# A pre-norm attention and gated MLP block on one core: the exponentials of the last keys on VectorE as three shifted terms

## The chip, the core and the metric

The kernel runs on one core of a Trainium2 chip. TensorE multiplies matrices into PSUM, ScalarE takes exponentials, VectorE and GpSimd work element by element, and SyncE issues nearly all DMAs. The metric is the device time of one launch in microseconds (us), the median of the runs.

## The reference

One transformer block over 2048 rows of width 640, in bfloat16, with 32 heads of 20 columns:

```python
def _A_ref(x, wqkv, wo):
    qkv = (x @ wqkv).reshape(B, S, 3, H, Dh) ...
    scores = jnp.einsum("bhqd,bhkd->bhqk", q, k) * (Dh ** -0.5)
    p = _softmax(scores, axis=-1)
    o = jnp.einsum("bhqk,bhkd->bhqd", p, v)
    return o ... .reshape(B, S, D) @ wo
def _B_ref(x, w_gate, w_up, w_down):
    return ((x @ w_gate) * (x @ w_up)) @ w_down
h = x + _A_ref(_layernorm(x), wqkv, wo)
out = h + _B_ref(_layernorm(h), w_gate, w_up, w_down)
```

The hidden width of the second part is 1728.

## The kernel before

The 2048 queries are four blocks of 512 (block 0 to block 3), the heads eight groups of four. One **segment** is a block or half a block of queries with one group of heads; it runs over all 16 key tiles of 128 keys. Blocks 1, 2 and 3 take their first 4, 2 and 2 groups whole and the others in halves of 256 queries (passes C and D, E and F, A and B), so that the rows of a first half can go on early. A **unit** is one key tile (two in a half) by one head, 128 x 512 scores, one bank of PSUM.

Most units go to ScalarE: three and two banks in turn make a score tile `sc`, one activation turns it into `E`. The rest go to VectorE, 12 of the 64 units of a whole segment (`D_WHOLE`) and 6 of the 32 of a half (`D_HALF`), the last ones in key order. There the exponential is built from integer bits: a `TENSOR_SCALAR` from PSUM into `di` (L744), and for each pair of units three operations more (`dm` L627, `dt` L629, their product L632). `dt` and `di` are two terms whose sum is the exponential, so TensorE multiplies both with V into `acc` (L871). The sums of each row come from a column of ones in V; `norm` sends them through DRAM, takes their inverse on GpSimd (`rr`, L769), spreads it (`bc`) and scales there (L784).

When a block's or a half's groups are normed, its **tail** follows as jobs in one queue: `load`, `out` (output product, residual, layer norm, transposes), `glu` (up and gate products with weights `wu`, `wg`, or `wres` that stay in SBUF) and `y` (down product, store). Block 0 has one tail of 512 rows, the others have tails of 256 rows, and the last 256 rows have `last_tail` after everything.

All instructions are written out once by a planner that keeps clocks for the engines (`clk`). Per score tile `emit_S` issues scores and activation, then `fill_step` issues products with V and pieces of jobs on TensorE until shortly before ScalarE will want the next scores; where there is nothing to do, `idle_products` issues products that are thrown away. So each engine's order is fixed before the run. What is still in the queue after the last score tile comes out behind it, ahead of `last_tail`. `by_cols` splits TensorE work into strips of 32 columns.

Of the kernel before, what the change touches and what calls it, by code (L numbers as in the profile page):

```python
# [18 lines left out]
P = 128  # L19
# [25 lines left out]
D_WHOLE = (12, 12, 12, 12)  # L45
# [19 lines left out]
EXP_BIAS = KAPPA - 127.0 * math.log(2.0)  # L65
DB = 2
# [21 lines left out]
def kernel(  # L88
# [178 lines left out]
    clk = {"pe": 0.0, "dve": 0.0, "acc": 0.0, "kind": None, "piece": ROUND}  # L267
# [155 lines left out]
    TAILS = [(0, list(range(TPB)), [("0", range(NG))])]  # L423
# [21 lines left out]

    a_units, d_units, due, left = [], [], [], {}
    for s, (p, g, lo, hi, _) in enumerate(segs):
# [10 lines left out]
        left[s] = [n * (sum(u[2] == j for u in units) + sum(u[2] == j for u in own)) for j in range(HPG)]  # L458

    LAST_B, LAST_T = NB - 1, [2, 3]  # L460
    first_b = [next(k for k, u in enumerate(us) if all(PASS[segs[v[0]][0]][0] == LAST_B for v in us[k:])) for us in (a_units, d_units)]
    pos = {"a": 0, "d": 0}
# [15 lines left out]
    dve_now = {"tile": None, "n": 0, "us": [], "key": 0}  # L478
# [163 lines left out]

    def step_dq():
# [31 lines left out]
    def take(i):  # L675
# [4 lines left out]
        if late_d and (not wide or due[di] + 4 <= ia):  # L680
            when = max(clk["pe"], act_end.get(i - 2, 0))
            ok = next_free() < when + 200 or due[di] + LEAD < ia
            for k in range(di, di + 4):
                if ok and k < len(d_units) and d_units[k][0] == d_units[di][0] and all(d_units[k][2] != u[2] for u in us):
                    d_units[di], d_units[k] = d_units[k], d_units[di]
                    d = d_units[di]
                    pos["d"] += 1
                    break
# [3 lines left out]
    def emit_S(i):  # L692
# [9 lines left out]
        if d and dve_now["tile"] is None:  # L702
# [39 lines left out]
        if d:  # L742
# [87 lines left out]
    def when(u):  # L830
        return u[0] if u[4][0] == "d" else act_end[u[0]] + WAKE

    def pick(s, i, flush, need):
        units = list(av_d[s]) + list(av_a[s])
        fit = lambda u: u[0] <= (clk["pe"] if u[4][0] == "d" else i - 2)
# [5 lines left out]
        for u in first + rest:  # L841
            if u[2] not in seen and len(got) < HPG:
                seen.add(u[2])
                got.append((av_d[s] if u[4][0] == "d" else av_a[s], u))
        return got

    def emit_AV(i, rounds, flush=False, need=None):
        while rounds > 0 and acc["next"] < len(segs):
# [15 lines left out]
            for q, u in got:  # L864
                q.remove(u)
                _, kt, j, e, owner = u
# [231 lines left out]

# [3 lines left out]
    def open_late():  # L1102
# [6 lines left out]
        late["s"] = pool("ls", 2, side="right")  # L1109
        late["if"] = late["s"].tile([P, P], F32, name="identf", bufs=1)  # L1110
# [9 lines left out]
    def new_st(rows_of):  # L1120
        hp = late["h"]
        st = {"rows": rows_of, "xr": {}}
        st["ln2T"] = hp.tile([P, KT, QB], BF16, name="ln2T")
        st["hh"] = [hp.tile([P, 2, QB], BF16, name=f"hh{f}") for f in range(FP)]
# [436 lines left out]
```

## Time and profile before

| what | value |
|---|---|
| runs | 876.83, 881.02, 881.36 us; median 881.02 |
| profiled execution, span from first to last instruction | 875.8 us, mean granted clock 0.991 |
| its own time beside the span | not among the times shown; the runs lie 1.0 to 5.6 us above the span |
| busy: TensorE, ScalarE, VectorE, GpSimd | 827.1, 799.6, 701.5, 191.0 us |
| exponentials on ScalarE | 679 activations, the first at 29.14 us, the last ending at 820.8 us |
| units on VectorE | 350 in 175 pairs |

Line numbers (L744) are those of the kernel before. In rows of groups the columns are: line, engine, operation, output and inputs, shapes, count, then busy time in us and mean ns of one, then the idle time before them and what ended it. In rows of the timeline: start and length in us, engine, line, operation, count; an entry in brackets is idle time before. In rows of windows: the stretch, its length, busy time and count of each engine, the granted clock, the share of the DMA engines and GB/s. A busy TensorE row is not TensorE at its peak, since its matmuls overlap; times per matmul are therefore read from rows of weight loads (PEld) in an unbroken run.

### The profile page before, as it was taken

The numbers are of one execution on the slowest core, as the hardware profiler recorded it, in microseconds if no ns is written. First come the engines' busy times: TensorE is split into PE (matmuls) and PEld (weight loads), VectorE is DVE, ScalarE is ACT, GpSimd is POOL, SyncE is SP. The second block draws the span as 40 slices with busy tenths as digits, with TensorE's granted clock in tenths as the row PEclk, the third lists the DMA queues.
The fourth block names the chain that finished last, engine by engine and source line by source line (L and its number), as shares of the span: only waits on it lengthen the run. The fifth ranks groups of instructions, "written<-read, shape, count | busy, mean of one in ns | idle before, by whom it ended". The sixth has DMA issues, their size and how long they took to land.

```text
span 875.8 us, 34459 instructions
## 1 busy us (share of the span) xinstructions
PE 827.1 (94%) x15313; PEld 406.3 (46%) x15313; DVE 701.5 (80%) x1384; ACT 799.6 (91%) x711; POOL 191.0 (22%) x259
## 2 busy tenths in 40 slices
PE   8899999998999999999999999999999999999995
PEld 5334334332334334445444555655454556555774
DVE  6675778899778989888888888989988898788632
ACT  5899999999999999999999999999999999899530
POOL 2220001344413322212230223122310232014000
PEclk9999999999999999999999999999999999899998
DMA  6111230144222322101314031413510310031310
GB/s 183 35 59 52 68 98 3 44 120 114 53 67 53 115 74 76 39 9 39 98 40 128 24 98 45 117 31 97 127 34 23 99 48 15 17 93 48 82 46 18
DMA packets 93959, 57.62 MB, mean 66 GB/s; under 512 B 24236, under 2 KB 91692, under 8 KB 93804
## 3 DMA queue, kind: packets, MB, share of 16 engines
q1 hardware_dynamic: 93804, 55.36, 23.7%
q8 instruction: 121, 1.98, 0.9%
q14 instruction: 34, 0.28, 0.1%
HBM read 46.94 MB, written 8.16 MB: 63 GB/s over the span
## 4 chain that ended last, share of the span: by engine, by line
PE 46%; ACT 25%; DVE 19%; issue 5%; DMA 2%; SPq 1%; POOL 1%; ACTq 0%; DVEq 0%; POOLq 0%
ACT E L732 25%; PE sc L724 11%; PE acc L871 9%; PE mi L286 9%; PE mi L1214 8%; DVE di L744 5%; PE mi L360 3%; DVE di L632 2%; DVE dm L627 2%; DVE st L219 2%; PE f L286 2%; PE f L1214 2%; DVE dt L629 2%; PE mi L724 1%; PE acc L1421 1%
## 5 line engine op out<-in xcount | busy, mean ns | idle before, releaser
L732 ACT ACTIVATE E<-sc 128x1536 bf16<-128x1536 f32 (+1 forms) x679 | 782.5, 1271 | 23.6 <-PE sc L724 10.6
L744 DVE TENSOR_SCALAR di<-mi 128x512 int16<-128x512 f32 x350 | 238.1, 685 | 65.9 <-PE mi L724 61.8
L871 PE MATMUL acc<-E,vx 128*32 128x256 bf16 (+1 forms) x2532 | 221.4, 315 | 2.6 <-DVE vx L257 2.0
L724 PE MATMUL sc<-qa,kT 21*128 21x256 bf16 (+1 forms) x1800 | 205.2, 320 | 15.0 <-ACT E L732 10.1
L724 PEld LDWEIGHTS <-kT 21*128 21x128 bf16 x3072 | 85.6, 92 | 218.9 <-issue 208.7
L769 POOL TENSOR_TENSOR rr<-rr,powers 128x8 f32<-128x8 f32 (+1 forms) x44 | 95.9, 2180 | 407.0 <-DMA rr<-sums 406.9
L871 PEld LDWEIGHTS <-vx 128*32 128x32 bf16 x3612 | 81.5, 95 | 105.7 <-issue 95.0
L632 DVE TENSOR_TENSOR di<-di,dm 128x1024 bf16<-128x1024 bf16 x175 | 122.2, 698 | 4.6
L724 PE MATMUL mi<-qa,kT 21*128 21x256 bf16 (+1 forms) x376 | 98.0, 311 | 2.4 <-DVE di L744 1.3
L627 DVE TENSOR_SCALAR dm<-di 128x1024 int16<-128x1024 int16 x175 | 77.7, 444 | 3.7
L871 PE MATMUL acc<-dt,vx 128*32 128x256 bf16 (+1 forms) x540 | 78.1, 311 | 0.5 <-DVE dt L629 0.4
L871 PE MATMUL acc<-di,vx 128*32 128x256 bf16 (+1 forms) x540 | 77.8, 308 | 0.8 <-DVE di L632 0.6
L629 DVE TENSOR_SCALAR dt<-di 128x1024 int16<-128x1024 int16 x175 | 76.2, 436 | 0.0
L724 PE MATMUL sc<-qb,kT 21*128 21x256 bf16 (+1 forms) x732 | 67.1, 291 | 2.8 <-ACT E L732 2.4
L286 PE MATMUL mi<-wd,hh 128*32 128x320 bf16 x1344 | 63.5, 305 | 0.4 <-DVE hh L1239 0.2
L1214 PE MATMUL mi<-ln2T,wg 128*32 128x256 bf16 (+1 forms) x1170 | 55.6, 298 | 1.9 <-DVE di L744 1.0
L1214 PE MATMUL mi<-ln2T,wu 128*32 128x256 bf16 (+1 forms) x1170 | 54.6, 298 | 0.9 <-DVE di L744 0.5
L286 PEld LDWEIGHTS <-hh 128*32 128x32 bf16 (+1 forms) x1456 | 46.1, 98 | 18.0 <-issue 7.5
L1214 PEld LDWEIGHTS <-wg 128*32 128x32 bf16 (+1 forms) x1190 | 32.6, 96 | 13.7 <-issue 10.0
L286 PE MATMUL mi<-kT,ident 128*32 128x512 bf16 x528 | 37.0, 382 | 1.7 <-DVE di L744 1.6
L1214 PEld LDWEIGHTS <-wu 128*32 128x32 bf16 (+1 forms) x1190 | 32.4, 96 | 13.3 <-issue 9.3
L257 DVE CAST u<-mi 128x512 bf16<-128x512 f32 x49 | 33.5, 683 | 4.9 <-PE mi L1214 4.8
(134 smaller groups left out, 794.1 us busy)
## 6 DMA issues: line engine op xcount, KB each, us to landing
wu<-in_B_w_up_dram SPq DMA_DIRECT2D x29, 320.0 KB
wg<-in_B_w_gate_dram SPq DMA_DIRECT2D x29, 320.0 KB
dense<-dn SPq DMA_DIRECT2D x36, 128.0 KB
bc<-scr SPq DMA_DIRECT2D x64, 64.0 KB
bc<-scr SPq DMA_DIRECT2D x112, 32.0 KB
xr<-in_A_x_dram SPq DMA_DIRECT2D x16, 160.0 KB
out_dram<-xr SPq DMA_DIRECT2D x14, 160.0 KB
wd<-in_B_w_down_dram SPq DMA_DIRECT2D x13, 160.0 KB
```

The costliest lines, as they stand in the source:

```text
L257: nc.vector.tensor_copy(dst, src)
L286: nc.tensor.matmul(out[k:k + w, :], lhsT=lhsT[:, k:k + w], rhs=rhs, **flags)
L360: nc.tensor.matmul(ps[k:k + SLOT, :], lhsT=wqk_half(c, col // HALF)[:, m, col % HALF:col % HALF + SLOT], rhs=lnT[:, c, ch * QB:(ch + 1) * ...
L627: nc.vector.tensor_scalar(m16[:, 0:n], s16, M_MASK, M_BITS, ALU.bitwise_and, ALU.bitwise_or)
L629: nc.vector.tensor_scalar(t16[:, 0:n], s16, E_MASK, E_BITS, ALU.bitwise_and, ALU.bitwise_or)
L632: nc.vector.tensor_tensor(sb[:, 0:n], sb[:, 0:n], mb[:, 0:n], ALU.mult)
L724: nc.tensor.matmul(dst[:, h * w:(h + 1) * w], lhsT=kT[g][SLOT * j:SLOT * j + VS, (kt + h) * P:(kt + h + 1) * P], rhs=q_of(g, b, c0, w)[SLO ...
L732: nc.scalar.activation(e[:, 0:n], sc[:, 0:n], ACT.Exp, bias=EXP_BIAS, scale=SM_SCALE)
L744: nc.vector.tensor_scalar(t[:, k * BANK:(k + 1) * BANK], sd[:], EXP_A, 0.0, ALU.mult, ALU.max)
L769: nc.gpsimd.tensor_tensor(ri, r16, powers[:, 1:2].to_broadcast([P, n]), ALU.pow)
L871: nc.tensor.matmul(acc["t"][SLOT * j:SLOT * (j + 1), 0:w], lhsT=vx[kt][:, VS * h:VS * h + SLOT], rhs=e, start=(j not in acc["new"]), stop= ...
L1214: nc.tensor.matmul(ps[r0 + x:r0 + x + d, col:col + n], lhsT=wt[:, c, f0 + x:f0 + x + d], rhs=st["ln2T"][:, c, c0:c0 + n], start=(c == 0), ...
```

## The change

In blocks 1 and 2 the exponentials of key tiles 14 and 15 that go to VectorE are made in another way: VectorE makes one integer tile `pt`, GpSimd adds 42 and 85 to it for two more terms, and all three, read as bfloat16, are multiplied with copies of V that carry a weight each. GpSimd writes these weighted copies once, after block 0's scores, into the space of block 0's queries. That is 48 of the units of whole segments and 80 of the halves, 128 in all; 246 stay with the old way. Whole segments of blocks 1 and 2 give VectorE 16 units in place of 12, 24 more in all. The rule by which a tile picks its VectorE unit looks further ahead. Block 0's tail becomes two of 256 rows, buffers of the tails shrink to that, their opening moves ahead of block 1, and the resident weights wait until block 2's products with V are done.

```diff
-D_WHOLE = (12, 12, 12, 12)
+D_WHOLE = (12, 16, 16, 12)
+STEPS = (0, 42, 85)
+WEIGHTS = (0.478515625, 0.3828125, 0.30859375)
+SUM_T = (14, 15)
+SUM_B = (1, 2)
+SUM_BUFS = 3
+POOL_ADD = 650
...
-    TAILS = [(0, list(range(TPB)), [("0", range(NG))])]
+    TAILS = [(0, [2 * k, 2 * k + 1], [("0", range(NG))]) for k in range(2)]
...
+    def summed(u):
+        s, kt, j = u
+        return PASS[segs[s][0]][0] in SUM_B and kt in SUM_T
...
+    def scale_values():
+        for kt in SUM_T:
+            for k, w in enumerate(WEIGHTS):
...
+                    nc.gpsimd.tensor_scalar(qa_all[:, g, x:x + n * VS], vx[kt][:, h * VS:(h + n) * VS], w, None, ALU.mult)
...
+    def three_terms(t, u, key):
...
+        clk["pool"] = max(clk["pool"], clk["dve"] + 150)
+        for k in range(3):
+            if k:
+                nc.gpsimd.tensor_scalar(t[:, k, :], t[:, 0, :], STEPS[k], None, ALU.add)
+                clk["pool"] += POOL_ADD
+            at = clk["pool"] if k else clk["dve"]
+            for h in range(BANK // w):
+                av_d[s].append((at + 250, kt + h, j, t[:, k, h * w:(h + 1) * w].bitcast(BF16), ("p", key), k))
...
+        three = d and summed(d)
+        if three:
+            ensure(("open",))
+            p_key = dve_now["p"] = dve_now["p"] + 1
+            free_of(("p", p_key - SUM_BUFS))
+            t3 = late["p"].tile([P, 3, BANK], I16, name="pt", bufs=SUM_BUFS)
...
+        if three:
+            nc.vector.tensor_scalar(t3[:, 0, :], sd[:], EXP_A, 0.0, ALU.mult, ALU.max)
+            ev(BANK)
+            three_terms(t3, d, p_key)
...
+                v = scaled(u[5], kt, h) if len(u) > 5 else vx[kt][:, VS * h:VS * h + SLOT]
                 nc.tensor.matmul(
-                    acc["t"][SLOT * j:SLOT * (j + 1), 0:w],
-                    lhsT=vx[kt][:, VS * h:VS * h + SLOT], rhs=e,
+                    acc["t"][SLOT * j:SLOT * j + v.shape[1], 0:w], lhsT=v, rhs=e,
...
-        if not seen["last"] and pos["a"] >= first_b[0] and pos["d"] >= first_b[1]:
+        if not seen["last"] and pos["a"] >= first_b[0] and pos["d"] >= first_b[1] and acc["next"] >= last_seg:
```

How instructions move, at three places (line numbers after the change are higher; buffer numbers stand behind the names). First GpSimd, from the norm of block 0's last group into block 1. Before, with the inverse (`rr`), the scaling into `on` or `part` and the note of the sums:

```order
L769 TENSOR_TENSOR rr_4742<-rr_4742,powers_186 128x16
L784 TENSOR_TENSOR on7_145<-asb1_4740,bc0_4989 128x512
L753 TENSOR_TENSOR seen_sums_109<-seen_sums_109,rr_4742 128x32
L1113 MEMSET wd13_5233 64x640
L1125 MEMSET hh6_5242 64x512
L769 TENSOR_TENSOR rr_5166<-rr_5166,powers_186 128x16
```

The same place on GpSimd after the change, where `pt` are the tiles of three terms:

```order
L830 TENSOR_TENSOR rr_4796<-rr_4796,powers_186 128x16
L679 TENSOR_SCALAR pt_4927<-pt_4927 128x512 x2
L679 TENSOR_SCALAR pt_4953<-pt_4953 128x512 x2
L679 TENSOR_SCALAR pt_4970<-pt_4970 128x512 x2
L679 TENSOR_SCALAR pt_5009<-pt_5009 128x512 x2
L679 TENSOR_SCALAR pt_5029<-pt_5029 128x512 x2
L679 TENSOR_SCALAR pt_5051<-pt_5051 128x512 x2
L679 TENSOR_SCALAR pt_5073<-pt_5073 128x512 x2
L679 TENSOR_SCALAR pt_5090<-pt_5090 128x512 x2
L845 TENSOR_TENSOR on7_145<-asb1_4794,bc0_5063 128x512
L814 TENSOR_TENSOR seen_sums_109<-seen_sums_109,rr_4796 128x32
L830 TENSOR_TENSOR rr_5207<-rr_5207,powers_186 128x16
```

Sixteen adds, for eight units, now stand between the inverse of one norm and its scaling.

Second VectorE in the first segments of block 1, before (pairs of units with their three operations):

```order
L744 TENSOR_SCALAR di_5989<-mi_5991 128x512
L744 TENSOR_SCALAR di_5989<-mi_6013 128x512
L629 TENSOR_SCALAR dt_5987<-di_5909 128x1024
L632 TENSOR_TENSOR di_5909<-di_5909,dm_5986 128x1024
L744 TENSOR_SCALAR di_6077<-mi_6079 128x512
```

and VectorE there after the change:

```order
L644 TENSOR_TENSOR di_4885<-di_4885,dm_4938 128x1024
L800 TENSOR_SCALAR pt_5009<-mi_5011 128x512
L800 TENSOR_SCALAR pt_5029<-mi_5031 128x512
L800 TENSOR_SCALAR pt_5051<-mi_5053 128x512
L800 TENSOR_SCALAR pt_5073<-mi_5075 128x512
L800 TENSOR_SCALAR pt_5090<-mi_5092 128x512
L805 TENSOR_SCALAR di_5134<-mi_5136 128x512
```

A summed unit leaves VectorE one operation, and eight of them come in a row.

Third VectorE at the end, around the copy of the last segment's product (`asb` from `acc`). `xr` takes the output product of a tail, `ln2` and `ln2T` its layer norm, each `u` and `hh` one of the seven steps of its GLU. Before, with the last pair's product first:

```order
L632 TENSOR_TENSOR di_20694<-di_20694,dm_20823 128x1024
L1246 TENSOR_TENSOR hh3_19383<-mi_20834,u_20814 128x2x256
L257 CAST u_20946<-mi_20905 128x512
L1246 TENSOR_TENSOR hh4_19384<-mi_20948,u_20946 128x2x256
L898 COPY asb0_21006<-acc_20668 128x128
L257 CAST u_21050<-mi_21009 128x512
L1246 TENSOR_TENSOR hh5_19385<-mi_21052,u_21050 128x2x256
L257 CAST u_21135<-mi_21094 128x512
L1239 TENSOR_TENSOR hh6_19386<-mi_21094,u_21135 64x256
```

After the change, from that copy on:

```order
L959 COPY asb0_21164<-acc_20885 128x128
L1206 TENSOR_TENSOR xr_20914<-mi_21167,xr_20914 128x320
L1206 TENSOR_TENSOR xr_20914<-mi_21201,xr_20914 128x320
L226 BN_STATS st_21236<-xr_20912 128x6 x2
L227 BN_AGGR mv_21235<-st_21236 128x2
L226 BN_STATS st_21240<-xr_20914 128x6 x2
L227 BN_AGGR mv_21235<-st_21240 128x2
L250 TENSOR_SCALAR ln2_21254<-xr_20912,m32_21246,rstd_21252 128x640
L250 TENSOR_SCALAR ln2_21256<-xr_20914,m32_21246,rstd_21252 128x640
L264 COPY ln2T_20903<-mi_21258 128x5x128
L264 COPY ln2T_20903<-mi_21265 128x5x128
L264 CAST u_21313<-mi_21272 128x512
```

Before, the tail ahead of `last_tail` has two of its seven GLU steps left at this copy; after the change it has half of its output product, its layer norm and all seven steps still to come.

More of the change, by code (lines that the diff above doesn't have):

```diff
@@ L682, in take @@
             ok = next_free() < when + 200 or due[di] + LEAD < ia
[L683 to L685 removed]
+            same = [k for k in range(di, min(di + 16, len(d_units))) if d_units[k][0] == d_units[di][0]]
+            for k in sorted(same, key=lambda k: (-sum(d_units[x][2] == d_units[k][2] for x in same), k)) if ok else ():
+                near = a_units[ia:ia + len(us) + 4]
+                got = []
+                for u in near:
+                    if len(got) < len(us) and u[2] not in [d_units[k][2]] + [v[2] for v in got]:
+                        got.append(u)
+                if len(got) == len(us):
+                    us = got
+                    a_units[ia:ia + len(near)] = got + [u for u in near if u not in got]
+                    d_units.insert(di, d_units.pop(k))
                     d = d_units[di]
@@ L1109, in open_late @@
         late["s"] = pool("ls", 2, side="right")
+        late["p"] = pool("lp", side="right")
         late["if"] = late["s"].tile([P, P], F32, name="identf", bufs=1)
@@ L1122, in new_st @@
         st = {"rows": rows_of, "xr": {}}
-        st["ln2T"] = hp.tile([P, KT, QB], BF16, name="ln2T")
-        st["hh"] = [hp.tile([P, 2, QB], BF16, name=f"hh{f}") for f in range(FP)]
+        st["ln2T"] = hp.tile([P, KT, HW], BF16, name="ln2T")
+        st["hh"] = [hp.tile([P, 2, HW], BF16, name=f"hh{f}") for f in range(FP)]
         nc.gpsimd.memset(st["hh"][-1][M1:P, 1, :], 0.0)
@@ L1427, in idle_products @@
             mm(ROUND)
-    seen = {"t": 0, "last": False}
+    seen = {"t": 0, "last": False, "scaled": False}
     i = 0
@@ L1446 @@
             idle_products(i)
+        if not seen["scaled"] and all(PASS[segs[us[pos[x]][0]][0]][0] for x, us in (("a", a_units), ("d", d_units))):
+            scale_values()
+            seen["scaled"] = True
         i += 1
```

72 lines of the change are left out of this document (46 added, 26 removed).

## The prediction

> **What bounds the kernel now.** I read the page first: busy shares and the slices.
>
> ```profile
> span 875.8 us, 34459 instructions
> PE 827.1 (94%) x15313; PEld 406.3 (46%) x15313; DVE 701.5 (80%) x1384; ACT 799.6 (91%) x711; POOL 191.0 (22%) x259
> ACT  5899999999999999999999999999999999899530
> ```
>
> ScalarE is at 90% or more in nearly every slice up to the 37th, then stops: the run is a score phase and an end of TensorE work. Next, in the waits, who waits for whom in the score phase (total, times, longest):
>
> ```profile
> PE sc L724 <- ACT E L732: 12.5, 46, 0.7
> ACT E L732 <- PE sc L724: 10.6, 21, 1.5
> ACT E L732 <- PE mi L724: 9.5, 24, 1.3
> ```
>
> The two wait for each other by turns and never long: TensorE's fillers are planned to end just as ScalarE frees its tile. Third, the timeline for ScalarE's pace (start, length, count), from its first exponential to the end of its last run:
>
> ```profile
> 29.14 1.45 ACT L732 ACTIVATE E<-sc 128x1536 bf16<-128x1536 f32 x1
> 129.25 39.60 ACT L732 ACTIVATE E<-sc 128x1024 bf16<-128x1024 f32 x35
> 228.96 69.99 ACT L732 ACTIVATE E<-sc 128x1536 bf16<-128x1536 f32 x61
> 815.93 4.85 ACT L732 ACTIVATE E<-sc 128x1024 bf16<-128x1024 f32 x4
> ```
>
> At its best it takes 39.60/35 = 1.131 us a tile (wide and narrow in turn, 2.5 banks on average); around block 1's start 69.99/61 = 1.147. The score phase is 820.8 - 29.1 = 791.6 us for 679 tiles, 1.166 each. Last, the timeline after the last score matmul:
>
> ```profile
> 818.89 0.39 PE L724 MATMUL sc<-qb,kT 21*128 21x256 bf16 x6
> 822.72 3.82 PEld L1214 LDWEIGHTS <-wres 128*32 128x32 bf16 x140
> 826.75 0.31 PE L1344 MATMUL f<-xr,ident 128*128 128x320 bf16 x1
> 832.46 7.57 PEld L286 LDWEIGHTS <-hh 128*128 128x128 bf16 x56
> ```
>
> From 818.89 to the first matmul of the last tail (L1344) are 7.9 us, filled with 240 GLU matmuls; from there to the end are 49.0 us, which the change leaves alone. So two things set the time: how long the score phase is, and how much of the tail before the last is still undone when it ends.
>
> **The change part by part.** *ScalarE.* The tiles go from 340 wide and 339 narrow to 335, 334 and one of a single bank: five pairs fewer at 2 x 1.131 = 2.26 us, one short one more (0.59 us, first row below): **-10.7 us** of score phase.
>
> ```profile
> L255 ACT CAST u<-f 128x512 bf16<-128x512 f32 x7 | 4.1, 585 | 10.6 <-PE f L1214 10.6
> L744 DVE TENSOR_SCALAR di<-mi 128x512 int16<-128x512 f32 x350 | 238.1, 685 | 65.9 <-PE mi L724 61.8 <-PE sc L724 2.5
> L632 DVE TENSOR_TENSOR di<-di,dm 128x1024 bf16<-128x1024 bf16 x175 | 122.2, 698 | 4.6
> L627 DVE TENSOR_SCALAR dm<-di 128x1024 int16<-128x1024 int16 x175 | 77.7, 444 | 3.7
> L629 DVE TENSOR_SCALAR dt<-di 128x1024 int16<-128x1024 int16 x175 | 76.2, 436 | 0.0
> L213 POOL COPY wp<-wqk 128x640 bf16<-128x640 bf16 x3 | 2.0, 719 | 3.9 <-DMA wqk<-in_A_wqkv_dram 3.9
> L228 POOL TENSOR_SCALAR ve<-mvb 128x2 bf16<-128x2 bf16 x7 | 2.1, 301 | 0.0
> L784 POOL TENSOR_TENSOR on<-asb,bc 128x512 bf16<-128x512 f32 x6 | 7.7, 1276 | 28.9 <-DMA bc<-scr 28.9
> L769 POOL TENSOR_TENSOR rr<-rr,powers 128x8 f32<-128x8 f32 x28 | 48.7, 1740 | 184.3 <-DMA rr<-sums 184.2
> L753 POOL TENSOR_TENSOR seen_sums<-seen_sums,rr 128x16 f32<-128x16 f32 x32 | 9.5, 296 | 34.4 <-DVE rr L800 34.4
> L1214 PE MATMUL mi<-ln2T,wg 128*32 128x256 bf16 x900 | 34.9, 274 | 0.9 <-DMA scr<-rr 0.5 <-DVE di L744 0.4
> L1214 PE MATMUL mi<-ln2T,wg 128*32 128x512 bf16 x270 | 20.7, 381 | 1.0 <-DVE di L744 0.7
> ```
>
> *VectorE.* 24 more reads of PSUM at 0.685 are +16.4 us; 52 batches fewer at 0.698 + 0.444 + 0.436 = 1.578 are -82.1: 66 us less work. ScalarE never waits for VectorE in the rows above, so I count no gain; as a bound, bringing the 323 tiles of blocks 1 and 2 from 1.166 down to 1.131 us would be worth 11 us.
>
> *TensorE.* A summed unit has three products in place of two, a unit taken from ScalarE two or three in place of one: in the order, 152 unit products of 512 columns more, or 304 of 256. A narrow strip of 256 columns takes 3.82/140 = 27.3 ns, so +8.3 us. The planner's idle products fall by the equal of 128 of 512 columns, -7.0 us. So TensorE has about as much to do as before, but the score phase is 10.7 us shorter: 10.7 + 8.3 - 7.0 = 12 us of it have to come out behind. The order shows the same from the other side: behind the last score matmul now stand 108 matmuls of the output product, 10 transposes and 540 GLU matmuls in place of 240. That is 108/4 strips x 0.135 (7.57/56, the whole array's 320 columns) = 3.65, and 300 x 27.3 ns = 8.2: 11.9 us.
>
> *The end, then.* Moved out of the score phase, this tail also shows its latency. The same layer norm stands in the trace once near the end:
>
> ```profile
> 786.99 0.48 DVE L1144 TENSOR_TENSOR xr<-mi,xr 128x320 bf16<-128x320 f32 x1
> 790.10 0.65 POOL L224 CAST mvb<-mv 128x4 bf16<-128x4 f32 x1
> 794.13 0.80 DVE L243 TENSOR_SCALAR ln<-xr,m,rstd 128x640 bf16<-128x640 bf16 x2
> 796.04 0.88 DVE L257 COPY ln2T<-mi 128x640 bf16<-128x640 bf16 x2
> ```
>
> From the last add to the second transpose copied are 796.92 - 786.99 = 9.9 us. Before, score matmuls covered them; behind the last score nothing does. Two smaller terms:
>
> ```profile
> 752.00:756.00 4.00, 4.00 (x50) 2.34 (x50) 2.91 (x8) 3.23 (x3) 1.27 (x3) 0.70 0.02 6
> 756.00:760.00 4.00, 4.00 (x62) 1.96 (x62) 2.81 (x6) 2.68 (x3) 0.00 (x0) 0.50 0.00 0
> 556.24 3.24 DMA wg<-in_B_w_gate_dram
> ```
>
> In these windows the granted clock (third number from the end) fell to 0.70 and 0.50: 0.3 x 4 + 0.5 x 4 = 3.2 us lost. A 9.9 us hole may bring the like: 0 to 3.2, I take 2. The GLU's third weight pair is fetched when the first is done with; a fetch takes 3.24 us, 80 matmuls of the second cover 2.2: 1 us. So from the last score matmul: 0.4 (itself) + 0.5 (18 products with V) + 3.65 + 9.9 + 540 x 0.0273 = 14.7 + 2 + 1 = 32.2 us in place of 7.9: **+24.3 us** (19.4 to 25.5, with 8 us of latency and neither small term as the low end).
>
> By the Trainium skill (TensorE: Matmul & The Clock Gate, Part 1) the array drops to half rate after an idle window of about 3.4 us and stays there for as long of activity; that would be 1.7 us, an estimate, for the 2 above.
>
> *GpSimd.* 256 adds of 128x512. The rows have no such add. From below: the copy, 0.719 x 512/640 = 0.58; from above: the two-operand product, 1.28. Nearest is the copy with its fixed part taken off (0.301 + 512/638 x 0.418 = 0.64); beside VectorE's work I take 0.65. In a whole group eight summed units come one a tile (eight pairs of adds stand in a row): 1.30 us against 1.16 a tile, 1.1 us behind at the end, and TensorE takes each term as soon as the planner thinks it ready: 6 groups x 1.1 = **+6.7 us**. In a half group eight adds (5.2) and a norm (1.74 + 0.30 + the 0.72 of the row below = 2.8) share 10.4 tiles (12.1 us): no cost. Bounds: 0 and, at 0.72, 13 us. The 12 scalings stand ahead of block 1's first adds, once; 0 to 6 us, taken as nothing, since most need only long finished score groups.
>
> VectorE and GpSimd disturb each other here (before, the second row takes 0.42 to 0.44):
>
> ```profile
> 814.39 0.72 POOL L784 TENSOR_TENSOR part<-asb,bc 128x256 bf16<-128x256 f32 x1
> 814.58 0.82 DVE L629 TENSOR_SCALAR dt<-di 128x1024 int16<-128x1024 int16 x1
> ```
>
> By the Trainium skill (SBUF — State Buffer, SBUF: two separate sides) whichever of the two starts first holds their shared ports for its whole instruction and the other waits, which speaks against adds on GpSimd; this pair agrees. With some 0.05 us of such waiting an add, an estimate, the 6.7 would be 11.5.
>
> *Tails of 256 rows, weights twice, earlier opening.* A GLU matmul of 512 columns is 20.7/270 = 77 ns busy, two of 256 are 78: nothing. The second fetch hides behind score work as in the later tails.
>
> Sum: -10.7 + 24.3 + 6.7 = +20.3. On this execution's span 875.8 that is 896; the median of the runs, 881.0, lies 5.2 above that span; what lies around a span I take as unchanged, so **901 us**.
>
> **The rivals.** *Late adds (0.16).* If an add takes 0.85, each whole group ends 8 x (1.70 - 1.16) = 4.3 us late, 26 us in all: 881 - 10.7 + 24.3 + 26 = 921. It decides from about 0.7 on. For it: the pair of rows above; against: the copy's row.
> *No change (0.05).* VectorE's 66 us do count and blocks 1 and 2 run at 1.131: -11 more, and no wait for GpSimd: 881 - 21.7 + 24.3 = 884.
> *Faster (0.04).* The light VectorE lets ScalarE run at 1.131 a tile in all of the score phase: 670 x 1.131 - 0.5 = 757 in place of 791.6, -34.4 + 24.3 = -10, 871. It decides once the phase loses less than 6 us over that pace (before: 24). For it: 24 us are there; against: they lie in blocks 0 and 3 too, which have the same VectorE work, and the waits name TensorE.
>
> **How the numbers follow.** The forecast has 0.75: 886 (end 19.4, 4 us of the pace regained, GpSimd at nothing) to 909 (end 25.5, GpSimd 13). The range takes in the late adds at 921: 886 to 922. A measurement of this kernel can tell about 0.5% (4.4 us) from no change: faster 0.04, same 0.05, slower 0.91.
>
> **What would show it.** Right: the last exponential ends some 4 to 9 us earlier than at 820.8; a hole of 8 to 10 us on TensorE after it, with layer norm on VectorE and GpSimd; 540 GLU matmuls in one piece; L1344's successor starts 30 us or more after the last score matmul; POOL adds at 0.6 to 0.7; VectorE 60 us less busy. Wrong: adds of 0.8 or more with TensorE waiting for them in blocks 1 and 2 (the late adds), or a score phase shorter by 20 us and more (no change, faster); the argument falls if the GLU behind the last score is short or its layer norm covered.

## The result and the profile after

The changed kernel takes **1127.5 us** (median of 4 runs, 1121.1 to 1131.4) against 881.2 for before: ratio **1.281**, 95% interval 1.275 to 1.288. The prediction was 901 (886 to 922). The direction was right, the size was wrong by more than 220 us. The page of after, the lines that answer those of before:

```profile
span 1127.5 us, 35851 instructions
PE 945.6 (84%) x15877; PEld 452.8 (40%) x15877; DVE 663.8 (59%) x1254; ACT 805.9 (71%) x702; POOL 575.7 (51%) x527
ACT  6999989793755656667657486677678999899211
PE 35%; POOL 33%; DVE 14%; ACT 9%; issue 4%; DMA 3%; SPq 1%; POOLq 0%; DVEq 0%; ACTq 0%
```

ScalarE, at nine tenths in nearly every slice before, is mostly at five to seven from the 10th slice to the 30th: these are blocks 1 and 2, the two with the sums. GpSimd has gone from 22% to 51% and is a third of the chain that ended last. The waits of after (engine, line, total, times, longest):

```profile
ACT E L789 <- PE mi L781: 150.5, 114, 10.3
PE acc L933 <- POOL pt L679: 123.9, 138, 7.4
POOL pt L679 <- DVE pt L800: 92.4, 29, 6.0
ACT E L789 <- PE sc L781: 90.6, 71, 6.6
```

Read them as one chain. The products with V (L933) wait for the adds of GpSimd (L679). TensorE's order is fixed before the run, so the score products behind such a product wait too, and ScalarE waits for those: 241 us (150.5 + 90.6) where it was 20 before. VectorE's next summed unit cannot be read before its score product is done, and so GpSimd itself idles for 92 us in between. The groups say why the adds are late (busy, mean ns of one, idle before):

```profile
L679 POOL TENSOR_SCALAR pt<-pt 128x512 int16<-128x512 int16 x256 | 378.0, 1502 | 92.9 <-DVE pt L800 92.4
L805 DVE TENSOR_SCALAR di<-mi 128x512 int16<-128x512 f32 x246 | 169.0, 690 | 106.2 <-PE mi L781 102.2 <-PE sc L781 2.2
L644 DVE TENSOR_TENSOR di<-di,dm 128x1024 bf16<-128x1024 bf16 x123 | 90.5, 736 | 3.0
L800 DVE TENSOR_SCALAR pt<-mi 128x512 int16<-128x512 f32 x128 | 87.7, 688 | 132.6 <-PE mi L781 112.7 <-POOL pt L679 10.9 <-issue 5.6
L641 DVE TENSOR_SCALAR dt<-di 128x1024 int16<-128x1024 int16 x123 | 56.3, 458 | 0.0
L639 DVE TENSOR_SCALAR dm<-di 128x1024 int16<-128x1024 int16 x123 | 55.0, 447 | 2.7
...
L670 POOL TENSOR_SCALAR qa<-vx 128x504 bf16<-128x504 bf16 x4 | 5.9, 1472 | 0.1
L670 POOL TENSOR_SCALAR qa<-vx 128x336 bf16<-128x336 bf16 x4 | 4.4, 1108 | 0.1
L670 POOL TENSOR_SCALAR qa<-vx 128x168 bf16<-128x168 bf16 x4 | 4.2, 1052 | 0.1
```

**An add takes 1.50 us, not 0.65.** 256 of them are 378 us of GpSimd where the prediction had 166. Where the time lies is read from the first and last starts of block 3's score products and from the first product of the last tail (tile f, from xr). For after and for before (min, median and max ns, first to last start):

```profile
L781 PE MATMUL sc<-qb,kT x732: 264/277/604, 838.9 to 1048.2; 21*128 21x256 bf16 x157, 21*128 21x512 bf16 x26
L1410 PE MATMUL f<-xr,ident x4: 296/299/309, 1078.2 to 1082.5; 128*128 128x320 bf16 x4
```

```profile
L724 PE MATMUL mi<-qb,kT x164: 264/277/416, 618.0 to 816.6; 21*128 21x256 bf16 x140, 21*128 21x512 bf16 x24
L724 PE MATMUL sc<-qb,kT x732: 264/277/417, 619.3 to 819.0; 21*128 21x256 bf16 x157, 21*128 21x512 bf16 x26
L1344 PE MATMUL f<-xr,ident x4: 297/299/310, 826.8 to 831.2; 128*128 128x320 bf16 x4
```

Block 3 begins 220.9 us later (838.9 against 618.0). Its own scores take 8.3 us longer (209.3 against 201.0), the way from the last score product to the last tail 22.2 us longer (30.0 against 7.8), and what follows is as long as before (49.3 and 49.0). That is the 251.7 us between the two spans. The same marks, read in the same way, carry the experiments. Each ratio is to runs of before made beside that kernel (their medians are 877.4 to 881.2 us); the marks and the end are those of one profiled execution, and a difference of a few microseconds between two of them is no more than runs of one kernel show.

| kernel | time, us | ratio to before (95%) | block 3 begins | last score | last tail | end |
|---|---|---|---|---|---|---|
| before | 881.2 | | 618.0 | 819.0 | 826.8 | 875.8 |
| after | 1127.5 | 1.281 (1.275 to 1.288) | 838.9 | 1048.2 | 1078.2 | 1127.5 |
| adds on VectorE | 941.1 | 1.072 (1.068 to 1.076) | 634.9 | 844.8 | 889.5 | 937.2 |
| no summed units | 898.0 | 1.025 (1.020 to 1.031) | 633.1 | 836.3 | 846.0 | 893.4 |
| planner told 1500 ns | 1068.3 | 1.218 (1.212 to 1.224) | 776.2 | 985.3 | 1015.0 | 1065.1 |
| one add a unit | 988.9 | 1.126 (1.122 to 1.130) | 703.5 | 905.6 | 937.9 | 987.5 |
| units interleaved, planner told | 1015.8 | 1.155 (1.149 to 1.161) | 745.1 | 947.5 | 969.5 | 1018.5 |
| adds packed in pairs, told 850 | 963.5 | 1.099 (1.093 to 1.105) | 669.7 | 875.8 | 909.6 | 958.0 |

### The profile page after: what moved, and what is told of

It is laid out like the page before. It is cut to its first block, busy times and chain, and to the rows that moved or that the text cites. A ratio compares the mean times of both kernels' runs of the same rounds, so it can differ in the third digit from the quotient of the medians.

```text
span 1127.5 us, 35851 instructions
## 1 busy us (share of the span) xinstructions
PE 945.6 (84%) x15877; PEld 452.8 (40%) x15877; DVE 663.8 (59%) x1254; ACT 805.9 (71%) x702; POOL 575.7 (51%) x527
## 4 chain that ended last, share of the span: by engine, by line
PE 35%; POOL 33%; DVE 14%; ACT 9%; issue 4%; DMA 3%; SPq 1%; POOLq 0%; DVEq 0%; ACTq 0%
POOL pt L679 28%; ACT E L789 9%; PE sc L781 9%; PE acc L933 7%; PE mi L1276 6%; PE mi L293 6%; DVE di L805 4%; POOL rr L830 2%; DVE pt L800 2%; PE f L1276 1%; PE mi L367 1%; PE f L293 1%; POOL qa L670 1%; DMA bc<-scr 1%; DVE di L644 1%
## 5 line engine op out<-in xcount | busy, mean ns | idle before, releaser
L789 ACT ACTIVATE E<-sc 128x1536 bf16<-128x1536 f32 (+1 forms) x670 | 788.5, 1246 | 246.2 <-PE mi L781 150.5
L679 POOL TENSOR_SCALAR pt<-pt 128x512 int16<-128x512 int16 x256 | 378.0, 1502 | 92.9 <-DVE pt L800 92.4
L933 PE MATMUL acc<-E,vx 128*32 128x256 bf16 (+1 forms) x2508 | 264.1, 339 | 6.2 <-DVE vx L264 5.3
L933 PE MATMUL acc<-pt,qa 128*32 128x256 bf16 (+1 forms) x624 | 130.5, 349 | 124.7 <-POOL pt L679 123.9
L805 DVE TENSOR_SCALAR di<-mi 128x512 int16<-128x512 f32 x246 | 169.0, 690 | 106.2 <-PE mi L781 102.2
L933 PEld LDWEIGHTS <-vx 128*32 128x32 bf16 x3220 | 85.6, 97 | 212.1 <-issue 199.3
L800 DVE TENSOR_SCALAR pt<-mi 128x512 int16<-128x512 f32 x128 | 87.7, 688 | 132.6 <-PE mi L781 112.7
L644 DVE TENSOR_TENSOR di<-di,dm 128x1024 bf16<-128x1024 bf16 x123 | 90.5, 736 | 3.0
L933 PEld LDWEIGHTS <-qa 128*32 128x32 bf16 x624 | 41.6, 100 | 74.2 <-issue 71.3
L1276 PE MATMUL mi<-ln2T,wu 128*32 128x256 bf16 x1440 | 68.8, 310 | 2.6 <-DMA wu<-in_B_w_up_dram 1.8
L1276 PE MATMUL mi<-ln2T,wg 128*32 128x256 bf16 x1440 | 67.6, 296 | 0.5 <-DMA wg<-in_B_w_gate_dram 0.5
L293 PEld LDWEIGHTS <-hh 128*32 128x32 bf16 (+1 forms) x1456 | 50.0, 104 | 23.5 <-issue 10.2
L639 DVE TENSOR_SCALAR dm<-di 128x1024 int16<-128x1024 int16 x123 | 55.0, 447 | 2.7
L641 DVE TENSOR_SCALAR dt<-di 128x1024 int16<-128x1024 int16 x123 | 56.3, 458 | 0.0
L933 PE MATMUL acc<-dt,vx 128*32 128x256 bf16 (+1 forms) x356 | 51.6, 329 | 0.3 <-DVE asb L962 0.2
```

The source lines that it names most:

```text
L293: nc.tensor.matmul(out[k:k + w, :], lhsT=lhsT[:, k:k + w], rhs=rhs, **flags)
L639: nc.vector.tensor_scalar(m16[:, 0:n], s16, M_MASK, M_BITS, ALU.bitwise_and, ALU.bitwise_or)
L641: nc.vector.tensor_scalar(t16[:, 0:n], s16, E_MASK, E_BITS, ALU.bitwise_and, ALU.bitwise_or)
L644: nc.vector.tensor_tensor(sb[:, 0:n], sb[:, 0:n], mb[:, 0:n], ALU.mult)
L679: nc.gpsimd.tensor_scalar(t[:, k, :], t[:, 0, :], STEPS[k], None, ALU.add)
L789: nc.scalar.activation(e[:, 0:n], sc[:, 0:n], ACT.Exp, bias=EXP_BIAS, scale=SM_SCALE)
```

## The experiments

**Adds on VectorE.** GpSimd is taken out, and everything else of the change stays:

```diff
-                nc.gpsimd.tensor_scalar(t[:, k, :], t[:, 0, :], STEPS[k], None, ALU.add)
-                clk["pool"] += POOL_ADD
-            at = clk["pool"] if k else clk["dve"]
+                nc.vector.tensor_scalar(t[:, k, :], t[:, 0, :], STEPS[k], None, ALU.add)
+                dve_op(BANK / 3.84 + 75)
+            at = clk["dve"]
```

> The 256 adds move from GpSimd to VectorE, with the planner counting them there; all else is the changed kernel. Theory (the adds on GpSimd, 1.49 us each where 0.65 was planned, cause the loss): VectorE adds take about 0.3 us, the waits of TensorE and ScalarE in blocks 1 and 2 go, and the time is 895 to 915, the rest over before being undone tail work behind the last score (here even the down product of the tail before it). Rival (the scheme of three products itself, or the earlier opening and the split tail, cause it): still above 1000.

941.1 us: 186 of the 246 us are gone, so the adds on GpSimd are the cause of these, though the kernel stays slower than expected. On VectorE the same instruction is a fifth as long (groups, from 256 us to block 3):

```profile
L679 DVE TENSOR_SCALAR pt<-pt 128x512 int16<-128x512 int16 x250 | 67.0, 310 | 4.3
```

The 61.4 us that its span has over before's are 16.9 before block 3, 8.9 in block 3 and 36.9 between the last score product and the last tail, less 1.3 behind. The expectation (895 to 915) left 14 to 34 us over before, all of it for undone work behind the last score. There are 36.9 there, and 25.8 ahead of it that it had not counted. In this kernel's order 972 products (GLU, down projection and output product) and the layer norm stand behind the last score, and TensorE waits 5.5 us for the norm and 3.1 for the residual add there.

**No summed units.** The other parts of the change by themselves: tails of 256 rows, earlier opening, the new rule for picking VectorE's units.

```diff
-D_WHOLE = (12, 16, 16, 12)
+D_WHOLE = (12, 12, 12, 12)
...
-SUM_B = (1, 2)
+SUM_B = ()
...
-            scale_values()
+            pass
```

> No summed units, no 24 more units, no weighted copies of V; what stays is the split tail of block 0, the earlier opening, the later resident weights and the new pick of VectorE's unit. Theory: 880 to 892, since none of these waits for GpSimd; 220 GLU matmuls behind the last score as against 240 before. Rival (opening and split tail): a good part of the 246 us stays, above 950.

898.0 us, above the theory's range: the parts priced at nothing cost 2.5% (2.0 to 3.1). Block 3 begins 15.1 us later than in before. Adds on VectorE bring it only 1.8 us later still, with 24 units fewer for ScalarE.

**The planner told the price.** Same work, but the order of products is laid out for adds of 1500 ns.

```diff
-POOL_ADD = 650
+POOL_ADD = 1500
```

> The planner is told 1500 ns for an add in place of 650; the work is the same. If the loss is only mistimed order (TensorE stands in its queue before terms that are planned too early), it goes: below 930. If GpSimd's capacity is the bound (256 x 1.49 = 381 us of adds, about 75 of norms, 14 of weighted copies in two blocks that last about 370 us otherwise): it stays at 1010 to 1100.

1068.3 us: the wrong number in the planner costs 59 us, GpSimd's time itself most of the rest. The stretch from 256 us to block 3, in after, with the planner told, and with adds on VectorE (length, then busy time of PE, PEld, DVE, ACT, POOL, the granted clock, DMA share and GB/s):

```profile
256.00:839.00 583.00, 453.42 (x7513) 206.55 (x7512) 274.45 (x478) 373.30 (x312) 458.67 (x350) 0.80 0.17 45
```

```profile
256.00:777.00 521.00, 421.04 (x7505) 201.56 (x7508) 276.54 (x481) 368.75 (x313) 458.75 (x348) 0.82 0.20 50
```

```profile
256.00:634.90 378.90, 360.24 (x7293) 178.41 (x7288) 316.87 (x717) 360.20 (x312) 90.14 (x98) 0.98 0.24 62
```

GpSimd has 459 us of work here, 80 more than the whole stretch takes with the adds elsewhere. No order of the other engines can be shorter than that; with the right price in the planner it is busy for 88% of the stretch, with the wrong one for 79%. TensorE is slower in the first two as well: its granted clock is 0.80 and 0.82 where it is 0.98 with the adds on VectorE, and it is busy for 453 us with 7513 products where 7293 took 360 there. How much of the delay goes through the clock was not measured apart.

**One add a unit.** The third term reads the second one's sum, so 128 adds are left out.

```diff
-                nc.gpsimd.tensor_scalar(t[:, k, :], t[:, 0, :], STEPS[k], None, ALU.add)
-                clk["pool"] += POOL_ADD
+                if k == 1:
+                    nc.gpsimd.tensor_scalar(t[:, k, :], t[:, 0, :], STEPS[k], None, ALU.add)
+                    clk["pool"] += POOL_ADD
...
-                av_d[s].append((at + 250, kt + h, j, t[:, k, h * w:(h + 1) * w].bitcast(BF16), ("p", key), k))
+                av_d[s].append((at + 250, kt + h, j, t[:, min(k, 1), h * w:(h + 1) * w].bitcast(BF16), ("p", key), k))
```

> The second add of each summed unit is left out and its first sum is used twice, so the output is not the reference's; products on TensorE are the same. GpSimd then has 190 us of adds in blocks 1 and 2. Capacity: it fits, apart from the runs of eight units (8 x 0.33 = 2.6 us late, six times): 905 to 940. If the cost comes from each term's wait as such and not from the sum of GpSimd's work, about half of the 246 us stays: 990 to 1030.

988.9 us, between the two expectations. GpSimd's work is far below the stretch's length now (278.2 us busy of 447.5), and still block 3 begins 69 us later than with adds on VectorE: the planner, which counts 650 here as in after, puts products ahead of their sums, and TensorE waits for them in 46 places in this stretch:

```profile
PE acc L934 <- POOL pt L680: 46.1, 46, 7.4
```

Both causes are at work; this run alone could not part them.

**The forms by themselves.** Behind the end of before's loop, 21 GpSimd instructions on a spare tile (one execution).

```diff
+        for _ in range(3):
+            nc.gpsimd.tensor_scalar(i16[:, 512:1024], i16[:, 0:512], 42, None, ALU.add)
...
```

> The kernel before, with 21 GpSimd instructions on a spare tile added behind the end of the loop, three of each of seven forms: an int16 tensor-scalar add of 512 and of 256 columns, a bf16 tensor-scalar product of 512, a bf16 tensor-tensor product of 512, a bf16 copy of 512, a float tensor-scalar product of 256 and an int32 tensor-scalar add of 256. Theory, the tensor-scalar form itself is slow on GpSimd: 1.4 to 1.5 us for 512 columns whatever the operation and type, half of that for 256, and the copy 0.55 to 0.62 us. Rival, the adds were slowed by VectorE, which was writing through the same port at the time: by themselves the adds take 0.6 to 0.8 us.

The groups of that stretch (us busy, mean ns of one):

```profile
L1376 POOL TENSOR_SCALAR E<-E 128x512 int16<-128x512 int16 x3 | 4.5, 1499 | 0.3
L1380 POOL TENSOR_SCALAR E<-E 128x512 bf16<-128x512 bf16 x3 | 4.5, 1494 | 0.2
L1382 POOL TENSOR_TENSOR E<-E 128x512 bf16<-128x512 bf16 x3 | 3.1, 1041 | 0.2
L1388 POOL TENSOR_SCALAR E<-E 128x256 int32<-128x256 int32 x3 | 2.6, 852 | 0.2
L1378 POOL TENSOR_SCALAR E<-E 128x256 int16<-128x256 int16 x3 | 2.5, 849 | 0.2
L1384 POOL COPY E<-E 128x512 bf16<-128x512 bf16 x3 | 1.8, 614 | 0.2
```

The theory holds, but for "half of that for 256": 512 columns take 1.50 us and 256 take 0.85, whatever the type and the operation, some 0.2 us and 2.5 ns a column. The copy is near what the prediction took it for (0.614 us against 0.58 and 0.64). The run has no add of the changed kernel in it, but VectorE was busy with other work for about half of the stretch, so it does not by itself rule out a disturbance by VectorE. The adds of after do. Their durations (min, median and max ns):

```profile
L679 POOL TENSOR_SCALAR pt<-pt x256: 1480/1487/1977, 261.6 to 846.1; 128x512 int16<-128x512 int16 x128
```

49 of the 256 have no instruction of VectorE at their side at all, and these take 1.480 to 1.509 us. So it is the form. The wrong step was to price one form by the other.

**Adds packed in pairs.** The planner told, and each add done as 256 int32 additions.

```diff
-POOL_ADD = 1500
+POOL_ADD = 850
...
-                nc.gpsimd.tensor_scalar(t[:, k, :], t[:, 0, :], STEPS[k], None, ALU.add)
+                nc.gpsimd.tensor_scalar(t[:, k, :].bitcast(I32), t[:, 0, :].bitcast(I32), STEPS[k] * 65537, None, ALU.add)
```

> The kernel whose planner knows the adds' price (1068.25 us), with each add done as 256 int32 additions that hold two 16-bit values each (whether the lower of the two keeps all its bits is left out of the question), at 850 ns by the measurement of the forms instead of 1490; the planner counts 850. GpSimd's work in blocks 1 and 2 falls from 458.7 to about 295 us, under the 386 us that these blocks take with the adds on VectorE. Theory, it is GpSimd's time alone that held the kernel: blocks 1 and 2 take 390 to 420 us and the time is 940 to 975 us. Rival, the way through a third engine (semaphores, three buffers, a shared port) costs as much as its time: blocks 1 and 2 take over 450 us and the time is over 1000 us.

963.5 us, in the theory's range: GpSimd's time is what held the kernel. What is left of the route through a third engine, once that engine has room, is 34.8 us at block 3 over the adds on VectorE (669.7 against 634.9).

```profile
256.00:671.40 415.40, 374.40 (x7431) 189.05 (x7431) 265.64 (x474) 364.21 (x313) 298.95 (x347) 0.94 0.24 63
```

**Sums spread in the segment.** First by the keys' tiles, with the planner told:

```diff
-SUM_T = (14, 15)
+SUM_T = (13, 15)
```

> The kernel whose planner knows the adds' price (1068.25 us), with the sums at the keys' tiles 13 and 15 instead of 14 and 15, so that a summed unit and a plain one of VectorE alternate through a segment's second half. Blocks 1 and 2 took 521 us there with GpSimd busy for 458.7 us, and 386 us with the adds on VectorE. Theory, the 62 us above GpSimd's own work are due to the sums standing together at a segment's end, so that GpSimd is idle in the rest: blocks 1 and 2 take 465 to 495 us and the time is 1010 to 1045 us. Rival, what holds is a chain at each unit (three buffers, VectorE's unit, two adds, products) that is as long wherever the units stand: 1055 us or more.

983.8 us (ratio 1.120, 1.113 to 1.126), below both ranges, but the run does not answer the question. In half-width segments a unit covers two key tiles and starts at an even one, so none starts at 13 or 15: this edit took the sums away from all 20 of them. What it shows is another thing: with the 96 adds of the six full-width segments alone, block 3 begins at 708.9, 74 us after the kernel with adds on VectorE. The question was put again with all 256 adds, by changing the order of a segment's units:

```diff
         own = units[cut:]
+        plain, sums = [u for u in own if not summed(u)], [u for u in own if summed(u)]
+        if sums and plain:
+            at = lambda part: [((k + 0.5) / len(part), u) for k, u in enumerate(part)]
+            own = [u for _, u in sorted(at(plain) + at(sums))]
```

> The kernel whose planner knows the adds' price (1068.25 us), with VectorE's units of each segment in another order: summed units and plain ones in turn instead of all plain ones first (8 and 8 in a full-width segment, 4 and 2 in a half-width one); 256 adds as before. There GpSimd was busy for 37 to 39 us of each 40 in half-width segments (400 to 520 us), but for 30 us of each 40 in full-width ones (280 to 400 and 520 to 600 us), where the sums stand together at the end. Theory, the bunching costs the idle quarter: with the sums spread GpSimd is busy for 36 us or more of 40 there too, blocks 1 and 2 take 475 to 495 us instead of 521, and the time is 1020 to 1045 us. Rival, GpSimd's idle time in full-width segments comes from something else (the wait for a sum to be consumed, or for the layer norm's transfers): 1055 us or more.

1015.8 us; blocks 1 and 2 end where the theory said (489 us from 256), the whole kernel came out 4 us below its range. Three windows from the kernel with the planner told, then two of this one, full-width segments in the first and last:

```profile
280.00:400.00 120.00, 91.98 (x1176) 34.91 (x1168) 67.35 (x116) 76.96 (x66) 90.90 (x66) 0.74 0.19 53
400.00:520.00 120.00, 105.36 (x2214) 57.03 (x2212) 64.61 (x115) 95.97 (x83) 115.44 (x90) 0.87 0.22 55
520.00:600.00 80.00, 59.57 (x772) 22.27 (x772) 43.97 (x75) 49.81 (x43) 65.05 (x48) 0.79 0.13 33
```

```profile
280.00:400.00 120.00, 95.87 (x1507) 40.67 (x1500) 75.32 (x130) 86.58 (x75) 107.58 (x77) 0.90 0.20 53
256.00:745.10 489.10, 410.04 (x7793) 201.18 (x7794) 283.33 (x490) 370.89 (x315) 463.86 (x350) 0.89 0.20 54
```

GpSimd goes from 76% of the full-width stretch (90.90 of 120) to 90%, and is at 95% over the whole of blocks 1 and 2 (463.86 of 489.1). There the kernel is bound by GpSimd, to within the other 5%. The granted clock rises with it, from 0.74 to 0.90 in the full-width stretch.

**The scaled copies moved to VectorE**, on top of the adds there:

```diff
-                    nc.gpsimd.tensor_scalar(qa_all[:, g, x:x + n * VS], vx[kt][:, h * VS:(h + n) * VS], w, None, ALU.mult)
+                    nc.vector.tensor_scalar(qa_all[:, g, x:x + n * VS], vx[kt][:, h * VS:(h + n) * VS], w, None, ALU.mult)
```

> The kernel with the adds on VectorE (941.08 us), with the 12 scaled copies of the values moved from GpSimd to VectorE too. On GpSimd the twelve stood for 14.1 us (242.97 to 257.07) ahead of the reciprocal of a layer norm (rr). Theory, that stretch delays the start of block 1: block 3 begins 4 to 12 us earlier than 634.9 us and the time is 929 to 937 us. Rival, the copies were hidden there: block 3 begins at 633 to 637 us, 938 to 944 us in all.

942.1 us (1.066 to 1.078 of before): the rival's time, and block 3 begins no earlier (637.3 against 634.9). The copies' 14.1 us on GpSimd were hidden with the adds elsewhere. On VectorE a copy is again a fifth as long:

```profile
L670 DVE TENSOR_SCALAR qa<-vx 128x504 bf16<-128x504 bf16 x4 | 1.1, 282 | 0.0
```

In after they stand just ahead of the first adds, on the engine that bounds; that part was not measured apart.

**The small parts.** Three edits of the kernel without summed units (898.0 us): the late pools opened with block 0's first tail as in before, the old rule for picking units, and both.

```diff
-    do(("open",), lambda: open_tails())
...
-        if key != (0, 0):
-            do(("load",) + key, lambda: loads(b, ts))
+        if key == (0, 0):
+            do(("open",), open_late)
+        do(("load",) + key, lambda: loads(b, ts))
```

> The kernel without summed units (898.03 us) with the late pools opened where they were before, together with the first tail of block 0, so that VectorE's copy of the identity, the opening's loads and the weights no longer stand in the start of block 1. Theory, the earlier opening costs time there (the identity copy was held 4.7 us by a transfer, and the transfers of the opening stand ahead of the layer norm's own): block 3 begins 6 to 14 us earlier than 633.1 us. But this order leaves 572 products of the gated layers and of the result behind the last score product where before leaves 240, some 11 us at before's 7.9 us for 240, so the time is 890 to 902 us in all. Rival, the opening's place costs nothing: block 3 begins at 631 to 635 us and the time is 903 us or more.

915.0 us (1.034 to 1.045 of before): a miss in the other direction. Block 3 begins later (639.0), not earlier. So beside the new pick rule the earlier opening is a gain, not a cost.

```diff
-            same = [k for k in range(di, min(di + 16, len(d_units))) if d_units[k][0] == d_units[di][0]]
...
+            for k in range(di, di + 4):
+                if ok and k < len(d_units) and d_units[k][0] == d_units[di][0] and all(d_units[k][2] != u[2] for u in us):
+                    d_units[di], d_units[k] = d_units[k], d_units[di]
```

> The kernel without summed units (898.03 us) with the rule of before that looks for a VectorE unit among the next four and does not exchange ScalarE's units. Theory, the new rule costs some microseconds of short waits of ScalarE in block 0 (140 to 182 us, about 4.5 us): 891 to 895 us. Rival, the rule is free and the waits come from the split tail: 897 to 900 us.

903.1 us (1.025 to 1.034): no gain, and the theory falls. It lies above the rival's range too, but the interval overlaps that of the kernel without summed units (1.020 to 1.031).

> Both of before's rules put back into the kernel without summed units: what is left of the change is the tail of block 0 in two parts of 256 rows (its weights fetched twice) and the resident weights that come one segment later. Theory, the opening and the pick rule are what the small parts cost: 880 to 888 us. Rival, the split tail is the cost: 893 us or more.

893.2 us (1.013 to 1.022): the rival's number. Block 0's tail in two parts of 256 rows, the second fetch of its weights and the resident weights one segment later cost 15 us by themselves (against 877.8 for before beside it). On top of that the new pick rule alone is 21.8 us more (915.0), the earlier opening alone 9.9 (903.1), and both together 4.8 (898.0), which the intervals do not separate from nothing. These parts do not add up; that they go with the order that the planner finds is likely, but was not shown. From 246 us to block 3 in before (first) and here:

```profile
246.00:618.00 372.00, 356.59 (x7230) 173.84 (x7223) 319.65 (x621) 365.67 (x319) 89.72 (x97) 1.00 0.25 67
```

```profile
246.00:623.40 377.40, 358.39 (x7710) 184.44 (x7710) 323.22 (x616) 365.98 (x318) 89.70 (x96) 1.00 0.30 77
```

480 more products of half the columns give TensorE 1.8 us more busy time and 10.6 us more of weight loads, and ScalarE waits 9.7 us for score products where it waited 4.3. The other 10 us of the span lie in block 3 (7 us) and between the last score and the last tail (5 us), less 1.5 behind. What holds them there stays open.

## Why the prediction was wrong

**The step that failed is the price of an add**: "Nearest is the copy with its fixed part taken off ...; beside VectorE's work I take 0.65", with the two-operand product's 1.28 "from above". The add took 1.50. In the sum the adds stood at +6.7 us, 13 at most; moving them away from GpSimd takes off 186. Both ends were rows of another operation: the one-operand arithmetic form is dearer on GpSimd than the two-operand one (1.49 against 1.04 in bf16), which "from above" had excluded. Copy and arithmetic are not one class.

The range failed a second time by itself: it ended at an add of 0.85, below the prediction's own upper row. At 1.28 the rival's formula gives 6 x 8 x (2.56 - 1.16) = 67 and 20 x (10.2 + 2.8 - 12.1) = 18, some 980 us, an estimate, where the range ended at 922.

**The working around it was sound.** The rival "late adds" decided from 0.7 us on and had a formula: six full-width segments with eight units each, 2 adds against 1.16 us a tile, and half-width ones with eight adds and 2.8 us of norm in 12.1 us. With the measured price this is 6 x 8 x (2.98 - 1.16) = 87 and 20 x (11.9 + 2.8 - 12.1) = 52, together 139 us; the kernel with the planner told begins block 3 141.3 us after the one with adds on VectorE, and the 96 adds of the full-width segments alone cost 74. For 0.867, the packed adds, it gives 6 x 8 x (1.73 - 1.16) = 27 and nothing for the half-width ones; measured 34.8. The parts agree less closely than the sum (87 against 74, 27 against 34.8), so the 139 beside 141.3 is in part luck. Had the rival stood at 1.5, its price would have been 139 and not 26.

**A second term was missing: the planner's own number.** The change tells the planner 650 ns. With 1500 block 3 begins 62.7 us earlier. The prediction took the two as one quantity. A product put into TensorE's queue ahead of its operand holds up what stands behind it: that is the wait of L933 for L679 above.

Block 3's later start, taken apart by the runs in one order (another order could share it out in another way): 618.0 to 633.1 the small parts (15.1), to 634.9 the adds at VectorE's price (1.8), to 745.1 GpSimd's time (110.2), to 776.2 the sums standing together at a segment's end (31.1), to 838.9 the mistimed order (62.7).

**ScalarE, -10.7 us: not seen.** The nine tiles are gone (670 of 679), but even with the adds on VectorE block 3 begins no earlier. From 256 us to block 3 it is busy for 5.2 us less than in the kernel without summed units (360.2 against 365.4), but waits 18.4 us for score products where it waits 10.0 there. TensorE's 152 more unit products are the likely reason; no run took them away alone.

**VectorE, 66 us less work and no gain: 56 measured, and no gain seen.** By the groups shown, reads of PSUM are 18.6 us more (16.4 predicted) and the batches 74.3 less (82.1 predicted). The three forms of a batch went from 444 to 447, from 436 to 458 and from 698 to 736 ns.

**The end, +24.3: right, +22.2 measured, by the mechanism that was named.** The timeline after the last score product (1048.2) shows the predicted pieces:

```profile
1050.89 2.40 PE L293 MATMUL mi<-wo,part 128*32 128x320 bf16 x61
1053.33 0.49 DVE L1206 TENSOR_TENSOR xr<-mi,xr 128x320 bf16<-128x320 f32 x1 [0.59 <-PE mi L293]
1058.15 0.80 DVE L250 TENSOR_SCALAR ln<-xr,m,rstd 128x640 bf16<-128x640 bf16 x2 [2.31 <-POOL rstd L239]
1058.66 1.25 PE L330 MATMUL mi<-ident,ln 128*128 128x128 bf16 x10 [5.37 <-DVE ln L250]
1059.41 1.03 DVE L264 COPY ln2T<-mi 128x640 bf16<-128x640 bf16 x2 [0.46 <-PE mi L330]
1060.49 2.32 PE L1276 MATMUL mi<-ln2T,wu 128*32 128x256 bf16 x40 [0.58 <-DVE ln2T L264]
1062.58 1.92 PE L1276 MATMUL mi<-ln2T,wg 128*32 128x256 bf16 x40
1064.32 1.27 PE L1276 MATMUL mi<-ln2T,wu 128*32 128x256 bf16 x40
1065.41 1.27 PE L1276 MATMUL mi<-ln2T,wg 128*32 128x256 bf16 x40
1068.04 1.28 PE L1276 MATMUL mi<-ln2T,wg 128*32 128x256 bf16 x40 [0.26 <-DMA wg<-in_B_w_gate_dram]
```

The last add of the output product starts 5.1 us after the last score product (4.6 predicted), the layer norm takes 7.1 us from the last add to the second copy (9.9 predicted), and the GLU from 1060.49 to 1078.2 takes 17.7 us (14.7 + 2 + 1 predicted), with the fetch waited for by 0.26 us (1 predicted). The clock:

```profile
1056.00:1060.00 4.00, 1.25 (x10) 1.09 (x11) 1.35 (x4) 0.00 (x0) 1.90 (x5) 0.63 0.00 0
1060.00:1064.00 4.00, 3.51 (x69) 2.96 (x72) 1.13 (x2) 0.00 (x0) 0.00 (x0) 0.51 0.03 6
```

The granted clock is 0.37 x 4 + 0.49 x 4 = 3.4 us short here, where 2 was taken and 3.2 the bound. But TensorE was idle for most of the first window. What it cost is seen in the products: from start to start the first two groups of 40 take 2.09 and 1.74 us, the third 1.09, so some 1.7 us were lost, near the 2.

**Split tail, earlier opening and weights twice, "nothing": wrong**, 15.1 us at block 3 and 17.6 in the span. The split tail, with its second fetch and the later resident weights, is 15.3 of the span alone. "A GLU matmul of 512 columns is 20.7/270 = 77 ns busy, two of 256 are 78" is right for the busy time; it leaves out the weight loads (10.6 us more), the second fetch and the order. Which of these holds the 15 us is open.

**The scalings, "nothing" with 0 to 6.** A copy of 504 columns took 1.47 us and the twelve 14.5 us (5.9 + 4.4 + 4.2), most of it by the same form price; with the adds on VectorE they are hidden.

## What to carry to other kernels

Price an instruction on GpSimd by a row of the same form (copy, one operand with a constant, two operands), and where there is none, take no other form as a bound: three of them beside a running kernel cost a few microseconds to measure. Then compare the helper engine's whole work with the length of the stretch that it must fit in; above it, the engine is the new bound, and below it the bunching inside a segment and the planner's own price for it still decide some tens of microseconds. A formula with a threshold ("it decides from about 0.7 on") is worth evaluating at twice the price as well as just past the threshold.

## What the runs showed of the hardware

GpSimd's one-operand arithmetic with a constant takes 849 ns for 256 columns of int16 and 852 ns for 256 of int32, and 1.49 to 1.50 us for 512 of int16 or bf16. In these runs the price goes by the element and not by the byte, so the same values packed in pairs into 32-bit elements cost little more than half (867 ns in place of 1502 in the kernels). Whether the lower value of a pair keeps all its bits is left open. VectorE does the same 512 columns in 310 ns and a scaled copy of 504 in 282, where GpSimd takes 1472.

The adds in after are 1502 ns on average, against 1499 in the run of the forms. The Trainium skill (SBUF — State Buffer, SBUF: two separate sides) has the two engines wait for each other at their shared ports, where VectorE's instruction is in a mode that uses both of its port pairs or reads two operands from SBUF. The trace agrees: 21 of the 256 adds take more than 1.52 us, up to 1.98, and 18 of these overlap one of the three operations of a batch (L639, L641, L644), against 7 of the other 235. In all that is 4 us of the 378. On VectorE's side the three operations are 3, 22 and 38 ns longer than in before.

The scaled copies show it more plainly. 168 columns took 1052 ns on average in after, where the line through the forms' two lengths (0.2 us and 2.5 ns a column) gives 0.63 us. The kernel with units interleaved has the same twelve copies (min, median and max ns):

```profile
L674 POOL TENSOR_SCALAR qa<-vx x12: 628/1054/1692, 245.9 to 257.7; 128x504 bf16<-128x504 bf16 x4, 128x168 bf16<-128x168 bf16 x4, 128x336 bf16<-128x336 bf16 x4
```

There the two copies of 168 columns that overlap no operation of a batch take 628 ns each, as the line has it (the other two 779 and 628). In after all four overlap one and take 0.87 to 1.29 us.
